# Re-layout reads in 8 transfers per chunk in place of 12, and one transposing transfer per block in place of two

## The chip, the cores and the metric

The kernel runs on 1 core of one Trainium2 chip. The metric is the device time of that core in microseconds (us). The kernel before took 1019.06 us, the median of three runs (1019.06, 1015.35, 1019.22).

## The reference

One transformer block on 2048 tokens of width 640, in float32: a pre-norm attention with 32 heads of 20 over a sliding window of 256 tokens, then a pre-norm GEGLU feed-forward layer of width 1536.

```python
def _A_ref(x, wqkv, wo):
    B, S, D = x.shape
    H = 32; Dh = D // H; W = 256
    qkv = (x @ wqkv).reshape(B, S, 3, H, Dh).transpose(2, 0, 3, 1, 4)
    q, k, v = qkv[0], qkv[1], qkv[2]
    scores = einsum("bhqd,bhkd->bhqk", q, k) * (Dh ** -0.5)
    mask = (idx[:, None] - idx[None, :] >= 0) & (idx[:, None] - idx[None, :] < W)
    p = softmax(where(mask, scores, -1e9))
    o = einsum("bhqk,bhkd->bhqd", p, v)
    return o.transpose(0, 2, 1, 3).reshape(B, S, D) @ wo
...
h = x + _A_ref(layernorm(x), wqkv, wo)
h2 = h + (gelu(layernorm(h) @ w_gate) * (layernorm(h) @ w_up)) @ w_down
```

## The kernel before

**Tiles and parts.** The 2048 tokens are 16 blocks of 128, taken two at a time as 8 chunks of 256 tokens in the attention, and four at a time as 4 chunks in the feed-forward layer. Most products are made from float16 pairs: a value is split into a high part and a low part (what the high part misses), and a product is three matmuls (high by high, high by low, low by high).

**The path of one attention chunk.** `x_lane` normalises a block of x (`layernorm`), and for blocks 4 to 15 `turned` writes its high part (ScalarE) and its low part (VectorE) into one buffer `xp` and turns each with a transposing transfer into `xh` and `xl` (features on partitions). `qk` multiplies with the weights of q or k; `qk_out` splits the result into high and low and ScalarE writes it to a DRAM tile `qk` of [640 features, 2 parts, 256 tokens]. `stack` then reads this tile back in another layout: for each half of the heads (`par`, partitions 0 and 64) it puts three groups of 20 rows below one another, high, high, low for q (`qT`) and high, low, high for k (`kT`), so that one matmul over 60 rows gives all three products. That is 6 transfers of 20 rows x 16 heads x 256 tokens for q and 6 for k, 12 a chunk. Every transfer covers all 16 pairs of heads and both blocks.

**What uses it.** `maxima` multiplies qT with kT to get each row's maximum (VectorE reduces it), the negated maxima go through `max_transpose` as `mT` into rows 60 and 61 of each half of qT (two transfers of 2 rows from ScalarE's queue), `scores` then multiplies over 62 rows, ScalarE takes the exponential, GpSimd masks, and `value_lane` multiplies with v. `wo_block` applies the output weights, adds x, and writes h to DRAM.

**The feed-forward layer.** `norm_lane` reads h back, normalises it, and turns the high and low parts of a block with `turned` into two tiles, `h0h`/`h0l` or `h1h`/`h1l`, for chunks 1 to 3 (chunk 0 is turned on TensorE).

**What sets the order.** All engines' instructions are put in order when the program is built: a list scheduler (`Lane`, the loop at L1632) runs a model of the engines (`Clock`), in which a transfer costs by its bytes, and issues what that model holds ready. On the chip each engine executes its list in order and waits at semaphores. `stack` for chunk c may start once block 2c - 3 is scored (L772), since it overwrites the tiles which that block read, and in the model it keeps its transfers at most `PACE` apart from the line's end. All of its reads, the loads, the transposing transfers and the stores of h are issued by SP, on one queue; ScalarE issues the writes of `qk` and `mT` on another. Eight semaphores go round over the transfers of both queues, so a transfer waits until the one that last had its semaphore has landed.

Of the kernel before, what the change touches and what calls it, by code (L numbers as in the profile page):

```python
# [11 lines left out]
F32 = mybir.dt.float32  # L12
F16 = mybir.dt.float16
# [8 lines left out]
S, D, H, DH, F = 2048, 640, 32, 20, 1536  # L22
P = 128
NB = S // P
KC = D // P
G = 4
HG = H // G
CW = 2 * P
# [3 lines left out]
CB = 4  # L32
# [17 lines left out]
def _pow2(e):  # L50
    return float(2.0 ** e)
# [202 lines left out]
def block_kernel(ctx: ExitStack, tc: tile.TileContext, x, wqkv, wo, wg, wu, wd, out):  # L254
    nc = Clock(tc.nc)
# [3 lines left out]
    ffw = ctx.enter_context(tc.tile_pool(name="ffw", bufs=1))  # L259
# [50 lines left out]
    def need(*reads, slots=(), when=None, eng="tensor"):  # L310

        def f():
            if when and not when() or any(opened[n] >= banks[n] for n in slots):
                return INF
            return max([nc.ready(reads, eng)]
                       + [nc.slot(psums[n], n, banks[n]) for n in slots])
        return f
# [4 lines left out]
    def on(eng, *reads, when=None, after=None):  # L322
        f = need(*reads, when=when, eng=eng)
        if after is not None:
            return (eng,), lambda: max(f(), nc.others(after, eng))
        return (eng,), f
# [142 lines left out]
    def layernorm(xt, lane, hi, lo, dst=None, when=None, xn=None, e=XE, tp="tp",  # L469
                  dma=False):  # L470

        T = lambda n, *shape: nc.tile(lnp, [P] + list(shape), F32, n + lane)
        st = T("lst", 2, 6)
        for i in range(2):
            yield on("vector", xt)
            nc.vector.bn_stats(st[:, i, :], xt[:, i * 320:(i + 1) * 320])
        yield on("vector", st)
        mv = T("lmv", 2)
        nc.vector.bn_aggr(mv, st)
        yield on("vector", mv)  # L480
        ve = T("lve", 1)
        nc.vector.tensor_scalar(ve, mv[:, 1:2], EPS, None, op0=ALU.add)
        yield on("gpsimd", ve)

        y = T("ly", 1)
        a = T("lya", 1)
        nc.gpsimd.tensor_tensor(y, ve, mhalf, op=ALU.pow)
        yield on("vector", y)
        nc.vector.scalar_tensor_tensor(a, y, ve, y, op0=ALU.mult, op1=ALU.mult)
        yield on("vector", a)  # L490
        nc.vector.tensor_scalar(a, a, -0.5 * _pow2(e), 1.5 * _pow2(e), op0=ALU.mult, op1=ALU.add)
        yield on("vector", a)
        nc.vector.tensor_tensor(y, y, a, op=ALU.mult)
        yield on("vector", y)
        xn = xn()
        nc.vector.tensor_scalar(xn, xt, mv[:, 0:1], y, op0=ALU.subtract, op1=ALU.mult)
        if dma is not False:
            yield from turned(xn, lane, (hi, lo), dst, when, dma)
            return
        yield pe(xn, slots=[tp], when=when)  # L500
        if dst:
            hi, lo = dst()
        yield from transpose_part(xn, hi, lo, 0, 4, tp)
        yield pe(xn, slots=[tp])
        yield from transpose_part(xn, hi, lo, 4, 5, tp)

    def turned(src, lane, to, dst=None, when=None, two=None):

        key = "xparts" if dst else "parts"
        yield on("scalar", src, when=lambda: not opened[key] and (not when or when()))  # L510
        opened[key] += 1
        two = (two if dst else lnbuf[2]).bitcast(F16)
        hi, lo = two[:, :D], two[:, D:]
        nc.scalar.copy(hi, src)
        yield on("vector", hi)
        nc.vector.tensor_tensor(lo, src, hi, op=ALU.subtract)
        if dst:
            to = dst()
        for o, i in zip(to, (hi, lo)):
            yield ("sync",), need(i, eng="sync")  # L520
            nc.sync.dma_start_transpose(o, i)
        opened[key] -= 1

    def transpose_part(src, hi, lo, c0, c1, tp="tp"):
# [60 lines left out]
    wq = wqp.enter_context(tc.tile_pool(name="wq", bufs=1, side="right"))  # L585
# [5 lines left out]
    rooms = {"k": gu.bitcast(F32)[:, :KC * D].rearrange("p (c f) -> p c f", f=D)}  # L591
    rooms["k"] = [rooms["k"][:, i] for i in range(KC)]
    x32 = gu.bitcast(F32)[:, KC * D:KC * (D + CW)].rearrange("p (c n) -> p c n", n=CW)
    rooms["v"] = [gu.bitcast(F32)[:, KC * (D + CW):KC * (D + CW) + D]]
    hT = {0: tuple(ffw.tile([P, KC * CB * P], F16, name=n) for n in ("h0h", "h0l"))}
    rooms["v"] += [t.bitcast(F32)[:, i * D:i * D + D] for t in hT[0] for i in range(2)]
    hT[0] = tuple(t.rearrange("p (c n) -> p c n", c=KC) for t in hT[0])
    gu = gu.rearrange("p (a c f) -> p a c f", c=KC, f=512)

    HB = P // 2  # L600
# [55 lines left out]
    def hpart(c, b):  # L656
        return tuple(t[:, :, b * P:(b + 1) * P] for t in hT[c])

    class Block:
        ready = False  # L660
        maxima = halves = v = 0
        h, turned, normed, full = None, False, False, False
# [7 lines left out]
    B = [Block() for _ in range(NB)]  # L670
# [6 lines left out]
    def x_lane(blocks, lane):  # L677

        for j in blocks:
            c = C[j // 2]  # L680
            if j > 1:
                yield on("vector", when=lambda: W["k" if j < NR else "v"].scaled)
            if j >= NR and j + 1 < NB:
                yield ("sync",), lambda: max(0.0, nc.slot(att, "xt", 2))
                load_x(j + 1)

            def dst():
                if j < 2:
                    return x32[:, :, B[j].cols], None
                return xparts(j)  # L690

            yield from layernorm(B[j].x, lane, None, None, dst,
                                 lambda: j < 6 or c.x or C[j // 2 - 3].used == 4,
                                 lambda: B[j].x, tp="rb" if j in (1, 3) else "tp",
                                 dma=j >= NR and at("xp", [P, D], F32, 1))
            if j < 2:
                B[j].full = True
                tasks.append(x_cast(j))
            else:
                B[j].ready = True  # L700

    def xparts(j):
        c = C[j // 2]
        if c.x is None:
            c.x = tuple(nc.tile(wq, [P, KC, CW], F16, n, 3) for n in ("xh", "xl"))
        return tuple(t[:, :, B[j].cols] for t in c.x)

    def x_cast(j):
# [62 lines left out]
    def stack(c, which, d):  # L771
        yield ("sync",), need(d, when=lambda: pos["big"] == 2 and (W["q"].ready if c < 2 else  # L772
                                                                B[2 * c - 3].scored), eng="sync")
        if which == 0:
            C[c].qT = at("qT", [P, H // 2, CW], F16)
            for b in (2 * c, 2 * c + 1):
                B[b].mx = at("mxs", [P, H], F32, 4)
            to = C[c].qT
        else:
            s = 2 * c % RK  # L780
            to = kT[:, :, s:s + 2, :].rearrange("p i r n -> p i (r n)")
        for par in range(2):
            for m, i in enumerate(((0, 0, 1), (0, 1, 0))[which]):
                rows = slice(64 * par + DH * m, 64 * par + DH * m + DH)
                if c > 1:
                    yield ("sync",), lambda: nc.moved["sync"] - PACE
                nc.sync.dma_start(to[rows], d.rearrange("(a d i) m n -> a m d i n", a=2,
                                                        d=DH)[par, i])
        C[c].stacked += 1
        if C[c].stacked == 2:  # L790
            for b in (2 * c, 2 * c + 1):
                for pr in range(0, H // 2, pairs(b)):
                    heapq.heappush(maxq, (b, pr))
# [326 lines left out]
    ffpools = [None, None]  # L1120
# [200 lines left out]
    def norm_start(c):  # L1321
        yield ("sync",), need(when=lambda: pos["gu", c - 2] == FG - 1 if c > 1 else (
            ffpools[0] and W["d", 0].ready and all(b.wrote for b in B[CB:2 * CB])), eng="sync")
        if c == 1:
            hT[1] = tuple(nc.tile(ffpools[0], [P, KC, CB * P], F16, n) for n in ("h1h", "h1l"))
            lnbuf.extend(nc.tile(stage, [P, D], F32, "wsl", SLICES) for _ in range(3))
        else:
            hT[c] = hT[c - 2]
        for i, n in enumerate("hi"):
            side.append((LATE, norm_lane(c, (i, i + 2), n, lnbuf[i])))  # L1330

    def norm_lane(c, bs, lane, t):
        for b in bs:
            j = c * CB + b
            yield ("sync",), lambda: nc.others(t, "sync")
            nc.sync.dma_start(t, h_dram[j * P:(j + 1) * P, :])
            yield from layernorm(t, lane, *hpart(c, b), xn=lambda: t, dma=True,
                                 when=lambda: c < 2 or pos["gu", c - 2] == FG)
            chunk[c] += 1
        if chunk[c] == CB:  # L1340
            side.append((LATE, token_sums(c)))
# [285 lines left out]
    rows = Lane(row_lane())  # L1627
# [89 lines left out]
```

## Time and profile before

| | |
|---|---|
| median of three runs | 1019.06 us |
| the profiled execution, by its own time | 1015.33 us |
| its span, first to last instruction | 1013.6 us |
| mean granted TensorE clock | 0.997 |
| DMA packets; bytes | 105834; 112.67 MB |
| span in which attention runs, read from the first and last uses of kT | 51.8 to 566.3 us |
| transfers qT<-qk and kT<-qk | 48 and 48, 160.0 KB each |
| transposing transfers (x; h) | 24; 24 |

PE is TensorE, PEld its weight loads, DVE VectorE, ACT ScalarE, POOL GpSimd, SP SyncE; a q behind a name (SPq, ACTq) is that engine's instruction queue, here where it issues transfers. Nearly all instructions are recorded by one helper, so all have line L199: groups are told apart by their tiles, written out<-in. A row of the timeline has the start, the time taken, the engine and the instruction, with xN for N merged ones, and in brackets the idle time before it and what ended it. A row of the waits has the total, the count and the longest, in us. A row of the windows has the stretch, its length, the busy time and count of PE, PEld, DVE, ACT and POOL, the granted clock, the mean busy share of the 16 DMA engines, and GB/s.

### The profile page before, as it was taken

How to read it: one execution, taken by the hardware profiler on the slowest of the kernel's cores; microseconds unless marked ns; L12 is line 12 of the kernel's file. 1: busy time of each engine (PE TensorE's matmuls, PEld its weight loads, DVE VectorE, ACT ScalarE, POOL GpSimd, SP SyncE). 2: the span in 40 equal slices, each digit the busy share in tenths (PEclk: the TensorE clock that was granted, in tenths of full speed). 3: DMA queues.
4: the chain of work that ended last, by engine and by line, in shares of the span. 5: the costliest groups of instructions: out<-in, count | busy, mean ns of one | idle time of the engine just before them, and what ended most of it. 6: DMA issues, size and time to landing. Idle time of an engine off the chain costs nothing.

```text
span 1013.6 us, 30516 instructions
## 1 busy us (share of the span) xinstructions
PE 996.3 (98%) x12798; PEld 696.4 (69%) x12798; DVE 754.7 (74%) x2212; ACT 442.5 (44%) x711; POOL 315.0 (31%) x504
## 2 busy tenths in 40 slices
PE   8999999999999999999999999999999999999998
PEld 7876777666666776776655654577777777777776
DVE  7888999786667877676688687798888875544553
ACT  5516666654555555554567634432222212221220
POOL 7004344643344333332345311254313300000000
PEclk9999999999999999999999999999999999999999
DMA  8658775291271714236004342323453542222211
GB/s 308 148 127 177 185 163 167 67 166 41 71 133 39 143 55 88 64 79 188 18 29 133 68 130 92 98 107 116 144 187 102 148 142 78 79 103 80 78 53 52
DMA packets 105834, 112.67 MB, mean 111 GB/s; under 512 B 38368, under 2 KB 79584, under 8 KB 105696
## 3 DMA queue, kind: packets, MB, share of 16 engines
q1 hardware_dynamic: 93600, 99.97, 36.7%
q10 hardware_dynamic: 12096, 10.75, 3.5%
q8 instruction: 100, 1.64, 0.7%
q14 instruction: 38, 0.31, 0.1%
HBM read 73.73 MB, written 28.84 MB: 101 GB/s over the span
## 4 chain that ended last, share of the span: by engine, by line
PE 86%; DVE 7%; DMA 3%; ACT 2%; issue 1%; SPq 1%; POOL 0%; ACTq 0%; DVEq 0%
PE mm L199 44%; PE pv L199 12%; PE ra L199 12%; PE rb L199 10%; PE tp L199 7%; DVE junk L199 1%; DMA kT<-qk 1%; SPq L199 1%; DVE am L199 1%; DMA wst<-in_wu_dram 1%; DMA qT<-in_wqkv_dram 1%; DMA wst<-in_wg_dram 1%; ACT pt L199 1%; DVE ht L199 0%; DVE w1l L199 0%
## 5 line engine op out<-in xcount | busy, mean ns | idle before, releaser
L199 POOL TENSOR_SCALAR_AFFINE_SELECT pt<-pt 128x512 f32<-128x512 f32 x352 | 174.8, 512 | 297.0 <-ACT pt L199 281.3
L199 DVE CUSTOM_DVE_ANT_0 junk<-rb,band 128x320 bf16<-128x320 f32 x228 | 111.5, 489 | 53.4 <-PE rb L199 48.8
L199 ACT ACTIVATE pt<-ra,esc 128x640 f32<-128x640 f32 (+2 forms) x132 | 100.6, 770 | 74.3 <-PE ra L199 69.3
L199 DVE CUSTOM_DVE_ANT_0 junk<-ra,band 128x320 bf16<-128x320 f32 x220 | 107.7, 489 | 33.2 <-PE ra L199 26.8
L199 ACT ACTIVATE pt<-rb,esc 128x640 f32<-128x640 f32 (+2 forms) x124 | 94.1, 764 | 82.4 <-PE rb L199 73.2
L199 PE MATMUL pv<-pt,v 128*21 128x128 f32 x2880 | 104.7, 279 | 0.0
L199 PEld LDWEIGHTS <-ah 128*128 128x128 f16 x768 | 75.1, 98 | 29.2 <-issue 1.9
L199 ACT ACTIVATE gel<-gel,ffk 128x512 f32<-128x512 f32 x36 | 26.0, 722 | 134.3 <-DVE gel L199 134.3
L199 PEld LDWEIGHTS pv<-pt,v 128*21 128x21 f32 x2880 | 70.0, 101 | 9.9 <-issue 1.0
L199 PEld LDWEIGHTS <-ws 128*128 128x128 f16 x720 | 70.5, 98 | 8.1
L199 PEld LDWEIGHTS <-qT 60*64 60x64 f16 x1280 | 29.8, 104 | 61.0 <-issue 51.9
L199 PEld LDWEIGHTS <-kT 62*64 62x64 f16 x2880 | 63.4, 107 | 11.2 <-issue 7.5
L199 PEld LDWEIGHTS <-gu 128*128 128x128 f16 x440 | 41.9, 98 | 36.1 <-issue 2.5
L199 DVE SCALAR_TENSOR_TENSOR ht<-mm,ffk,ht 128x320 f32<-128x320 f32 x96 | 52.1, 545 | 13.7 <-PE mm L199 11.8
L199 ACT CAST ah<-gel 128x512 f16<-128x512 f32 x48 | 29.6, 617 | 68.7 <-DVE gel L199 68.6
L199 PE MATMUL mm<-xh,w1h 128*128 128x256 f16 x200 | 54.6, 273 | 0.8 <-DVE qks L199 0.8
L199 PE MATMUL mm<-xl,w1h 128*128 128x256 f16 x200 | 54.7, 274 | 0.0
L199 PE MATMUL mm<-xh,w1l 128*128 128x256 f16 x200 | 54.6, 273 | 0.0
L199 POOL TENSOR_TENSOR gelt<-gelt 128x256 f32<-128x256 f32 x18 | 15.3, 852 | 112.0 <-ACT gelt L199 111.9
L199 PE MATMUL mm<-w3h,oh 128*128 128x320 f16 x160 | 48.3, 302 | 1.4 <-DVE qks L199 1.4
L199 PE MATMUL mm<-w3l,oh 128*128 128x320 f16 x160 | 48.2, 301 | 0.0
L199 PE MATMUL mm<-w3h,ol 128*128 128x320 f16 x160 | 48.1, 300 | 0.0
(313 smaller groups left out, 2562.6 us busy)
## 6 DMA issues: line engine op xcount, KB each, us to landing
ws<-wsums SPq DMA_DIRECT2D x24, 640.0 KB
qk<-qks ACTq DMA_DIRECT2D x32, 256.0 KB
qT<-qk SPq DMA_DIRECT2D x48, 160.0 KB
kT<-qk SPq DMA_DIRECT2D x48, 160.0 KB
wsums<-ws SPq DMA_DIRECT2D x12, 640.0 KB
ht<-in_x_dram SPq DMA_DIRECT2D x16, 320.0 KB
h_dram<-ht SPq DMA_DIRECT2D x16, 320.0 KB
ht<-h_dram SPq DMA_DIRECT2D x16, 320.0 KB
```

The lines of the kernel that those rows point to most:

```text
L199: r = real(*args, **kw)
```

## The change

`stack` makes 4 transfers in place of 6: of the three groups of 20 rows, two neighbours go as one transfer of 40 rows, the third alone. For q the first two groups are the same source rows (high, high), so the source is read with a leading axis of 2 and step 0; for k they are high and low, so the source is read with the part axis first. The high and low parts of x share one tile `xhl` of 10 slices (the five of `xh`, then the five of `xl`), and those of h one tile `h0` or `h1`, so `turned` issues one transposing transfer of 10 slices after both parts are written, in place of one of 5 slices after each.

```diff
-            yield from turned(xn, lane, (hi, lo), dst, when, dma)
+            yield from turned(xn, lane, hi, dst, when, dma)
...
         if dst:
-            to = dst()
-        for o, i in zip(to, (hi, lo)):
-            yield ("sync",), need(i, eng="sync")
-            nc.sync.dma_start_transpose(o, i)
+            dst()
+            to = dst.all()
+        yield ("sync",), need(two, eng="sync")
+        nc.sync.dma_start_transpose(to, two)
...
+            dst.all = lambda: c.both[:, :, B[j].cols]
...
-            c.x = tuple(nc.tile(wq, [P, KC, CW], F16, n, 3) for n in ("xh", "xl"))
+            c.both = nc.tile(wq, [P, 2 * KC, CW], F16, "xhl", 3)
+            c.x = c.both[:, :KC], c.both[:, KC:]
...
+        parts_ = d.rearrange("(a d i) m n -> a m d i n", a=2, d=DH)
         for par in range(2):
-            for m, i in enumerate(((0, 0, 1), (0, 1, 0))[which]):
-                rows = slice(64 * par + DH * m, 64 * par + DH * m + DH)
+            for m, n in ((0, 2), (2, 1)):
+                rows = slice(64 * par + DH * m, 64 * par + DH * (m + n))
+                if n == 2:
+                    src = parts_[par] if which else parts_[par, 0].unsqueeze(0).to_broadcast(
+                        [2, DH, H // 2, CW])
+                else:
+                    src = parts_[par, 1 - which]
                 if c > 1:
                     yield ("sync",), lambda: nc.moved["sync"] - PACE
-                nc.sync.dma_start(to[rows], d.rearrange("(a d i) m n -> a m d i n", a=2,
-                                                        d=DH)[par, i])
+                nc.sync.dma_start(to[rows], src)
...
-            hT[1] = tuple(nc.tile(ffpools[0], [P, KC, CB * P], F16, n) for n in ("h1h", "h1l"))
+            hB[1] = nc.tile(ffpools[0], [P, 2 * KC, CB * P], F16, "h1")
+            hT[1] = hB[1][:, :KC], hB[1][:, KC:]
...
-            yield from layernorm(t, lane, *hpart(c, b), xn=lambda: t, dma=True,
+            yield from layernorm(t, lane, hB[c % 2][:, :, b * P:(b + 1) * P], None,
+                                 xn=lambda: t, dma=True,
```

SP's rows for chunk 4, in the kernel before; qk_3249 and qk_4034 are the DRAM copies of its q and k, xh and xl the turned x of a later chunk:

```order
L199 DMA qT<-qk_3249 20x16x256 x6
L199 DMA kT<-qk_4034 20x16x256
L199 DMA_TRANSPOSE xh<-xp 128x5x128
L199 DMA_TRANSPOSE xl<-xp 128x5x128
L199 DMA xt<-in_x_dram 128x640
L199 DMA kT<-qk_4034 20x16x256 x5
```

The same place after the change, from the transposing transfer ahead of it; qk_3253 and qk_4019 are now the copies of q and k:

```order
L199 DMA_TRANSPOSE xhl<-xp 128x10x128
L199 DMA ht<-in_x_dram 128x640
L199 DMA xt<-in_x_dram 128x640
L199 DMA qT<-qk_3253 40x16x256
L199 DMA qT<-qk_3253 20x16x256
L199 DMA qT<-qk_3253 40x16x256
L199 DMA qT<-qk_3253 20x16x256
L199 DMA kT<-qk_4019 40x16x256
L199 DMA kT<-qk_4019 20x16x256
L199 DMA kT<-qk_4019 40x16x256
L199 DMA kT<-qk_4019 20x16x256
```

Twelve reads have become eight that alternate between 40 and 20 rows, and the transposing transfers that stood among the reads of k now stand ahead of the whole stack.

ScalarE's rows, with their waits, while chunk 3's stack is in flight after the change: it writes the copy of chunk 4's k (qk_4019) and takes the exponentials (pt) of the blocks in work. DMAHW names the semaphores that go round over all transfers:

```order
L199 DMA qk_4019<-qks 128x2x512 [waits DMAHW2_49,DVE_49]
L199 ACTIVATE pt<-rb,esc 128x2x320 [waits PE_49,Pool_49]
L199 CAST h_100<-tp 128x128 [waits PE_49]
L199 ACTIVATE qks<-mm 128x2x256 [waits DMAHW7_49,PE_49]
L199 ACTIVATE pt<-ra,esc 128x2x320 [waits PE_49]
L199 DMA qk_4019<-qks 128x2x512 [waits DMAHW4_49,DVE_49]
L199 ACTIVATE pt<-rb,esc 128x2x320 [waits PE_49,Pool_49]
L199 ACTIVATE qks<-mm 128x256 [waits DMAHW2_49,PE_49]
L199 ACTIVATE pt<-rb,esc 128x2x320 [waits PE_49]
L199 DMA qk_4019<-qks 128x512 [waits DMAHW7_49,DVE_49]
```

The same rows in the kernel before, from its first write of that copy (qk_4034):

```order
L199 DMA qk_4034<-qks 128x2x512 [waits DMAHW6_49,DVE_49]
L199 ACTIVATE pt<-rb,esc 128x2x320 [waits PE_49,Pool_49]
L199 CAST h0h<-tp 128x128 [waits PE_49]
L199 ACTIVATE pt<-rb,esc 128x2x320 [waits PE_49]
L199 ACTIVATE qks<-mm 128x2x256 [waits PE_49]
L199 ACTIVATE pt<-ra,esc 128x2x320 [waits PE_49,Pool_49]
L199 DMA qk_4034<-qks 128x2x512 [waits DMAHW0_49,DVE_49]
L199 ACTIVATE qks<-mm 128x256 [waits DMAHW6_49,PE_49]
L199 ACTIVATE pt<-rb,esc 128x2x320 [waits PE_49]
L199 DMA qk_4034<-qks 128x512 [waits DVE_49]
```

In both, the writes wait for a transfer that was issued up to eight earlier, and the exponentials behind them stand in the same queue; all three writes have such a wait after the change, two of the three had one in the kernel before.

More of the change, by code (lines that the diff above doesn't have):

```diff
@@ L594, in block_kernel @@
     rooms["v"] = [gu.bitcast(F32)[:, KC * (D + CW):KC * (D + CW) + D]]
-    hT = {0: tuple(ffw.tile([P, KC * CB * P], F16, name=n) for n in ("h0h", "h0l"))}
-    rooms["v"] += [t.bitcast(F32)[:, i * D:i * D + D] for t in hT[0] for i in range(2)]
-    hT[0] = tuple(t.rearrange("p (c n) -> p c n", c=KC) for t in hT[0])
+    h0 = ffw.tile([P, 2 * KC * CB * P], F16, name="h0")
+    rooms["v"] += [h0.bitcast(F32)[:, i * D:i * D + D] for i in range(4)]
+    hB = {0: h0.rearrange("p (c n) -> p c n", c=2 * KC)}
+    hT = {0: (hB[0][:, :KC], hB[0][:, KC:])}
     gu = gu.rearrange("p (a c f) -> p a c f", c=KC, f=512)
```

## The prediction

> **What bounds the kernel now.** First the page: engine shares and the chain that ended last.
>
> ```profile
> span 1013.6 us, 30516 instructions
> PE 996.3 (98%) x12798; PEld 696.4 (69%) x12798; DVE 754.7 (74%) x2212; ACT 442.5 (44%) x711; POOL 315.0 (31%) x504
> PE 86%; DVE 7%; DMA 3%; ACT 2%; issue 1%; SPq 1%; POOL 0%; ACTq 0%; DVEq 0%
> ```
>
> TensorE is busy for 996.3 of 1013.6 us and carries 86% of the chain. It executes its rows in order and the change leaves its matmuls as they are, so the time can fall only by what PE waits, 17.3 us of idle time at most, but it can rise by any wait that is put in. So next the list of PE's own waits, for those that end with a transfer.
>
> ```profile
> PE rb L199 <- DMA kT<-qk: 2.1, 1, 2.1
> PE ra L199 <- DMA kT<-qk: 1.4, 1, 1.4
> ```
>
> Both are the re-layout reads (a stack: qT and kT from their DRAM copy) that the change regroups; no row there names a transposed tile. The timelines show one of them, of chunk 4 (SP's queue, then PE).
>
> ```profile
> 272.21 4.72 SPq L199 DMA_DIRECT2D qT<-qk  x6
> 276.98 0.74 SPq L199 DMA_DIRECT2D kT<-qk  x1
> 279.12 1.24 SPq L199 DMA_TRANSPOSE xh<-xp  x1
> 280.99 1.64 SPq L199 DMA_TRANSPOSE xl<-xp  x1
> 283.31 9.72 SPq L199 DMA_DIRECT2D kT<-qk  x5
> ```
>
> ```profile
> 295.62 0.32 PE L199 MATMUL ra<-kT,qT 60*64 60x320 f16 x1
> 297.31 0.33 PE L199 MATMUL ra<-kT,qT 60*64 60x320 f16 x3 [1.37 <-DMA kT<-qk]
> ```
>
> SP starts reading chunk 4 at 272.21. PE's first maxima matmul of it stands 23.4 us later and still waits 1.37 us. So this stage has cover: PE work between the start of the stack and its first use. Every transfer covers all 16 head pairs, so the first maxima need all of them. The same distance for the first and last of the six chunks 2 to 7, and for chunk 0:
>
> ```profile
> 29.43 5.47 SPq L199 DMA_DIRECT2D qT<-qk  x6
> 51.81 0.31 PE L199 MATMUL ra<-kT,qT 60*64 60x128 f16 x8
> 119.78 3.16 SPq L199 DMA_DIRECT2D qT<-qk  x4
> 159.46 0.38 PE L199 MATMUL ra<-kT,qT 60*64 60x320 f16 x4
> 449.08 4.71 SPq L199 DMA_DIRECT2D qT<-qk  x6
> 476.56 0.33 PE L199 MATMUL rb<-kT,qT 60*64 60x320 f16 x4
> ```
>
> Chunk 2 has 39.7 us and chunk 7 27.5; read the same way, chunks 3 to 6 have 26.6, 23.4, 27.5 and 20.0. Together 164.7, less the waits in chunk 4: 162. In the changed order chunk 2 loses a few us of it, so I take 160.
>
> **The new transfers: how many DMA engines?** A transfer's speed hangs on how many of the 16 DMA engines it uses. Windows (last columns: granted clock, DMA share, GB/s) in which one kind moves nearly alone, and the issues behind the second and third:
>
> ```profile
> 6.00:8.00 2.00, 2.00 (x26) 2.00 (x25) 1.32 (x6) 0.48 (x1) 1.87 (x3) 1.00 1.01 358
> 42.00:43.00 1.00, 1.00 (x6) 0.71 (x5) 0.53 (x2) 0.48 (x2) 0.00 (x0) 1.00 0.60 170
> 160.90:161.80 0.90, 0.90 (x11) 0.81 (x9) 0.87 (x4) 0.79 (x2) 0.00 (x0) 1.00 0.08 18
> 397.00:403.00 6.00, 6.00 (x131) 4.10 (x131) 4.36 (x15) 3.47 (x6) 2.01 (x5) 1.00 0.78 124
> 40.14 4.83 SPq L199 DMA_DIRECT2D kT<-qk  x6
> 159.64 1.28 ACTq L199 DMA_DIRECT2D qT<-mT  x2
> ```
>
> At 6 us the first loads, of 128 rows, fill all engines (1.01, 358 GB/s). At 42 stack reads of 20 destination rows from 320 source rows hold 0.60, just under 10/16. At 160.9 the two mT writes, 32 source rows to 2 destination rows, hold 0.08, under 2/16. So a transfer is cut into equal shares along its outermost rows, and the side with the fewer rows decides: 128 gives 16, 20 and 320 give 10, 2 and 32 give 2. The diff builds the 40-row transfers with 40 destination rows but a source whose outermost count is 2 (a broadcast of two copies, or the m axis put first). By that reading they run on **two engines**. If destination rows alone decided, 40 would give 10 as before; the trace has no source smaller than its destination to settle it. I take two, as the small side decided in the mT row.
>
> The Trainium skill (DMA: Bandwidth & Descriptors, section "Why a DMA increments its semaphore by 16 and not by 1") says that the largest number up to 16 is taken that divides the slowest dimension of both sides; the 10 and the 2 above agree, and by it the new transfers have two engines.
>
> **The sum.** One pass of q or k now is 40, 20, 40, 20 rows with 16 runs of 512 B each. The two engines get 320 + 32 + 320 + 32 = 704 runs each; before, an engine got 6 x 32 = 192. The price of a run: 170 GB/s over 10 engines is 17 GB/s each, 512 B in 30 ns (42 us); 124 GB/s gives 41 ns when several transfers press (397 us); the mT pair, 16 KB in 0.9 us over two engines, gives 28 ns for 256 B. I take 30, nearest to two engines that write different rows; 28 and 41 are the bounds. So q and k need 2 x 704 x 30 ns = 42 us. With 2 us from issue to the first bytes and landing (mT: issued at 159.64, moving at 160.9) and an estimated 4 us of other traffic on the same two engines (0 to 6), a stack takes 48 us.
>
> - Chunks 2 to 7: the stack may start only when the block that last read its buffers is scored, a fixed place in PE's order, so a stall of one chunk doesn't widen the next one's cover. 6 x 48 - 160 = **128 us**.
> - Chunk 0: 29.43 + 48 = 77.4 against a first use at 51.81: **26 us**.
> - Chunk 1: its transfers queue behind chunk 0's on the two engines till about 76, then take 42 + 2: 120. Its first use (88.8 before, 37.0 after chunk 0's) would come at 114: **6 us**.
> - Clock: after chunk 4's wait PE ran a stretch at half clock:
>
> ```profile
> 297.60:301.00 3.40, 3.40 (x78) 2.42 (x67) 1.00 (x4) 0.79 (x1) 1.42 (x3) 0.50 0.74 199
> ```
>
> 3.4 us at 0.50 lose 1.7. Eight long stalls at about 2 us each: **16 us** (0 to 27).
> - Given back: the old kT waits, 2.1 + 1.4, and their 1.7: **-5 us**.
>
> Sum +171. The profiled execution took 1015.33 us, 1.7 beyond its span: 1186. The median of the runs shown, 1019.06, stands 0.4% above that execution; I forecast by the latter.
>
> With 28 ns, no other traffic and no clock loss: a stack 41.4, so 6 x 41.4 - 162 + 19 - 5 = +100. With 41 ns: a stack 66, so 396 - 160 + 44 + 20 + 27 - 5 = +322. These are the bounds, 1115 and 1337.
>
> **The parts costed at nothing.** SP's issues:
>
> ```profile
> L199 SPq DMA_DIRECT2D kT<-qk x48: 742/742/1563, 40.1 to 468.5; - x48
> L199 SPq DMA_TRANSPOSE xh<-xp x12: 1214/1388/2211, 46.0 to 349.5; - x12
> ```
>
> 32 fewer reads at 0.74 us and 24 fewer transposes at 1.4 save SP up to 57 us, less what the larger ones cost more (nothing to double). PE gets none of it: SP's issues run ahead of the bytes. A joined transpose moves the same bytes; its high part now waits for VectorE's low part, and the two issues were 1.9 us apart (279.12, 280.99), so one turning shifts by at most 1.9 us either way. PE never waited for a turned tile; without that cover 24 x 1.9 = 45 us. What queues behind the slow reads on SP (xt, ht, weights) is needed a block or more later. ScalarE's writes of the next qk also wait for landings in the same window of eight semaphores, and its exponentials stand behind them: rival B.
>
> **Rivals.**
> A. *Ten engines* (0.13), the other side: the new reads keep 10 engines because destination rows decide. Then the stack lands no later, chunk 4's wait and half clock go, and 1015.3 - 5.2 gives 1010 (1006 to 1019). For it: the 20-row row fits this reading too. Against it: the mT row, unless only destinations count. It decides at eight engines: with n of them a stack takes 77/n + 10 us (2560 runs shared by n, 128 as before, at 30 ns, and the 6 us above), 48 at two and 20, the smallest cover, at eight. The Trainium skill (same page, "Rules for kernel authors") advises joining many small transfers into one large one; by that alone this would be the outcome.
> B. *Two engines, and ScalarE held as well* (0.11): its qk writes wait for the 20-row reads that queue behind the 40-row ones, so about half of the cover runs after the landing instead of beside it: 1186 + 80 = 1266. For it: the waits in the order rows. Against: most of these writes stand late in the cover.
> C. *Mostly hidden* (0.04): two engines, but far more cover than counted, 1015 to 1085. The distances above speak against it.
>
> **How the numbers follow.** Forecast 0.72 at 1186, its own range 1115 to 1337; B lies within, A and C outside. The range 1095 to 1335 holds a little over 8 in 10. A measurement tells about 0.5% (5 us) from no change. A is split about evenly at that line: faster 0.06, same 0.08 (with a little of C), slower 0.86.
>
> **What would show it.** Right: in the windows right after a stack's issue a DMA share near 0.12 and some 35 GB/s for tens of us; PE's waits named kT<-qk or qT<-qk, eight of 6 to 30 us, each followed by a stretch at clock 0.5; the feed-forward stage after the last chunk as long as before. Wrong: a share near 0.6 during the stack, PE waits as before, and a span within 10 us. If PE waits for exponentials or qk tiles instead, rival B is at work.

## The result, and the profile after

The changed kernel takes **1190.71 us** (median of 6 runs, 1189.80 to 1193.33) against 1015.38 us for the kernel before in the same session (median of 6 runs). The ratio is 1.1718 with a 95% interval of 1.1692 to 1.1745: 17% slower. The prediction was 1186. Two single executions, one of 3413.85 us in experiment 8 and one of 1309.3 us of the kernel before measured beside it, lay far from all others of their kernels, and the ratios leave them out.

First the page of the changed kernel, the same lines as of the kernel before: span, busy time of the engines, the chain that ended last by engine.

```profile
span 1188.0 us, 30424 instructions
PE 1018.7 (86%) x12798; PEld 706.9 (60%) x12798; DVE 750.4 (63%) x2212; ACT 444.0 (37%) x711; POOL 312.8 (26%) x504
PE 63%; SPq 15%; DMA 12%; DVE 6%; ACT 2%; issue 1%; POOL 0%; ACTq 0%; DVEq 0%; POOLq 0%
```

The span grew by 1188.0 - 1013.6 = 174.4 us. PE executes the same 12798 matmuls. Its idle time is now 1188.0 - 1018.7 = 169.3 us where it was 17.3, so 152.0 us of the growth are waits; the other 22.4 us are busy time (1018.7 - 996.3), matmuls that ran slower. Of the chain, 27% now lie on SP's queue and the transfers (4% before), and PE's part fell from 86% to 63%. The list of PE's waits names what ended them (total, count, longest).

```profile
PE rb L199 <- DMA kT<-qk: 47.0, 6, 10.0
PE ra L199 <- DMA kT<-qk: 45.1, 5, 13.2
PE rb L199 <- ACT pt L199: 24.9, 4, 9.3
PE tp L199 <- ACT oT L199: 16.4, 1, 16.4
PE rb L199 <- DVE mxs L199: 9.3, 1, 9.3
PE ra L199 <- ACT pt L199: 7.0, 3, 6.4
```

The two kT waits, 3.5 us before, are 92.1 us now. Beside them stand waits for ScalarE and VectorE that hardly existed before. Windows tell how fast the transfers run: three stretches in which hardly anything but chunk 0's stack moves, then the feed-forward stage after the attention. The last three columns are granted clock, DMA share and GB/s.

```profile
43.00:45.00 2.00, 2.00 (x9) 1.43 (x8) 1.68 (x2) 2.00 (x5) 0.00 (x0) 1.00 0.14 39
45.00:47.00 2.00, 2.00 (x9) 1.42 (x8) 1.62 (x2) 1.14 (x3) 0.00 (x0) 1.00 0.14 43
53.00:55.00 2.00, 0.00 (x0) 0.00 (x0) 0.25 (x1) 0.00 (x0) 0.00 (x0) 1.00 0.14 44
740.00:1188.00 448.00, 442.63 (x3295) 307.16 (x3293) 315.67 (x657) 123.07 (x190) 92.36 (x94) 1.00 0.32 105
```

A share of 0.14 is 2.2 of 16 engines, at 17 to 20 GB/s each. Before, reads of this tile held 0.60 and 170 GB/s. In the feed-forward stage PE is idle for 448.00 - 442.63 = 5.4 us, as little as at the end of the kernel before, by its window:

```profile
575.00:1013.60 438.60, 433.20 (x3068) 300.14 (x3066) 307.33 (x631) 113.82 (x176) 87.21 (x80) 1.00 0.32 104
```

So the loss lies in the attention.

How one chunk shows it: SP's queue around chunk 4's stack (start, time taken), then PE's two waits in it, then a window behind the second.

```profile
360.74 18.49 SPq L199 DMA_DIRECT2D qT<-qk  x4
379.27 20.11 SPq L199 DMA_DIRECT2D kT<-qk  x4
```

```profile
384.71 0.48 PE L199 MATMUL ra<-qT,kT 62*64 62x128 f16 x12 [6.42 <-ACT pt L199]
394.98 0.44 PE L199 MATMUL rb<-kT,qT 60*64 60x320 f16 x1 [5.52 <-DMA kT<-qk]
```

```profile
394.60:401.40 6.80, 0.44 (x1) 0.12 (x1) 0.00 (x0) 0.00 (x0) 0.00 (x0) 0.50 0.22 58
```

The stack is issued at 360.74 and its first maxima start at 394.98; PE waits 6.42 us for an exponential and 5.52 for kT, then waits again, at a granted clock of 0.50. Six issues of q took SP 4.72 us before; four now take 18.49. Put together for all chunks, the windows from each stack's first issue to 20 us after its first maxima, of which the first two, the last, and the sum of the eight:

```profile
29.10:84.70 55.60, 33.05 (x276) 25.12 (x274) 24.18 (x89) 14.20 (x30) 1.65 (x3) 0.79 0.33 72
87.20:145.40 58.20, 38.78 (x439) 24.78 (x437) 27.98 (x120) 16.58 (x35) 8.94 (x12) 0.79 0.48 111
...
606.30:660.40 54.10, 37.82 (x613) 25.50 (x611) 20.54 (x78) 15.82 (x27) 9.77 (x21) 0.84 0.38 116
sum 453.60, PE 296.78 PEld 207.04 DVE 216.40 ACT 151.62 POOL 95.66; mean PE 37.10 PEld 25.88 DVE 27.05 ACT 18.95 POOL 11.96
```

Length less PE's busy time is its idle time: 22.6 us for chunk 0, 19.4 for chunk 1, 16.3 for chunk 7, and 453.60 - 296.78 = 156.8 for all eight, nearly all of the 169.3.

### The profile page after: what moved, and what is told of

Read it like the earlier page. It is cut to its first block, busy times and chain, and to the rows that moved or that the text cites. A ratio compares the mean times of both kernels' runs of the same rounds, so it can differ in the third digit from the quotient of the medians.

```text
span 1188.0 us, 30424 instructions
## 1 busy us (share of the span) xinstructions
PE 1018.7 (86%) x12798; PEld 706.9 (60%) x12798; DVE 750.4 (63%) x2212; ACT 444.0 (37%) x711; POOL 312.8 (26%) x504
## 4 chain that ended last, share of the span: by engine, by line
PE 63%; SPq 15%; DMA 12%; DVE 6%; ACT 2%; issue 1%; POOL 0%; ACTq 0%; DVEq 0%; POOLq 0%
PE mm L199 31%; SPq L199 15%; PE ra L199 9%; PE pv L199 9%; DMA kT<-qk 8%; PE rb L199 8%; PE tp L199 6%; DMA qT<-qk 2%; DMA xhl<-xp 1%; DVE junk L199 1%; DMA wsl<-in_wg_dram 1%; DVE ts L199 1%; DVE am L199 1%; ACT pt L199 1%; DVE w1l L199 0%
## 5 line engine op out<-in xcount | busy, mean ns | idle before, releaser
L199 DVE CUSTOM_DVE_ANT_0 junk<-rb,band 128x320 bf16<-128x320 f32 x214 | 104.7, 489 | 98.3 <-PE rb L199 93.0
L199 DVE CUSTOM_DVE_ANT_0 junk<-ra,band 128x320 bf16<-128x320 f32 x234 | 114.5, 489 | 82.3 <-PE ra L199 76.7
L199 PE MATMUL rb<-kT,qT 60*64 60x320 f16 (+4 forms) x616 | 40.8, 286 | 49.6 <-DMA kT<-qk 47.0
L199 PE MATMUL ra<-kT,qT 60*64 60x320 f16 (+4 forms) x664 | 44.1, 291 | 45.1 <-DMA kT<-qk 45.1
L199 PE MATMUL mm<-xhl,w1h 128*128 128x256 f16 x400 | 75.4, 282 | 1.2 <-DVE qks L199 1.2
L199 PE MATMUL rb<-qT,kT 62*64 62x128 f16 x1488 | 41.7, 214 | 34.2 <-ACT pt L199 24.9
L199 PE MATMUL mm<-xhl,w0h 128*128 128x256 f16 x350 | 66.8, 282 | 0.0
L199 PE MATMUL mm<-w2h,xhl 128*128 128x320 f16 x280 | 66.3, 316 | 0.0
L199 PE MATMUL mm<-h,gu 128*128 128x512 f16 (+1 forms) x272 | 65.8, 386 | 0.0
L199 PE MATMUL mm<-xhl,w1l 128*128 128x256 f16 x200 | 56.3, 282 | 0.0
```

Source lines behind the costliest of these rows:

```text
L199: r = real(*args, **kw)
```

## The experiments

The theory from the start: a 40-row read of the stack whose source has outermost count 2 runs on two DMA engines, and PE waits for the stack. Its main rivals: the joined reads are slow for another reason (their size, the order on SP's queue, the step-0 axis of q alone); the joined transposing transfers have a part; ScalarE, held by its writes, adds its own time. Ratios are to the kernel before, measured on the same chip in the same session.

**1. The joined reads alone.** `turned` and the tiles are those of the kernel before, `stack` is that of the change:

```diff
-        yield ("sync",), need(two, eng="sync")
-        nc.sync.dma_start_transpose(to, two)
+        for o, i in zip(to, (hi, lo)):
+            yield ("sync",), need(i, eng="sync")
+            nc.sync.dma_start_transpose(o, i)
...
```

> Only the joined re-layout reads, the turning transfers as before. Theory (a read whose source has an outermost count of 2 runs on two DMA engines, so a stack takes about 48 us): 1175 to 1205 us, and PE waits of about 20 us in each of the eight chunks. Rival (the joined transposing transfers are part of the loss): under 1170 us.

Measured: 1188.97 us (2 runs), ratio 1.1699 (1.1663 to 1.1736). The reads alone make the whole loss.

**2. The joined transposing transfers alone.** `stack` is that of the kernel before, with 12 reads:

```diff
-            for m, n in ((0, 2), (2, 1)):
+            for m, i in enumerate(((0, 0, 1), (0, 1, 0))[which]):
...
```

> Only the joined transposing transfers, the reads in 12 transfers of 20 rows as before. Theory: 1008 to 1020 us, the same as before within 0.5%. Rival (the joined turning delays x or h): over 1025 us.

Measured: 1010.66 us (6 runs), ratio 0.9944 (0.9924 to 0.9963), 0.6% below the kernel before: little, but the interval leaves out 1. The page of this kernel, and its waits for kT:

```profile
PE 992.2 (98%) x12798; PEld 694.6 (69%) x12798; DVE 750.8 (74%) x2212; ACT 444.5 (44%) x711; POOL 313.5 (31%) x504
```

```profile
PE rb L199 <- DMA kT<-qk: 1.7, 2, 1.2
PE ra L199 <- DMA kT<-qk: 0.3, 1, 0.3
```

Of the 4.7 us that the span lost (1013.6 to 1008.9), 4.1 are busy time of PE (996.3 to 992.2). The kernel before ran two stretches of 3.4 us at half clock, one after each kT wait of over a microsecond; the first of them:

```profile
229.55 0.32 PE L199 MATMUL rb<-kT,qT 60*64 60x64 f16 x3 [2.14 <-DMA kT<-qk]
```

```profile
229.30:232.70 3.40, 3.15 (x50) 1.77 (x50) 1.00 (x4) 0.79 (x1) 0.00 (x0) 0.50 0.03 7
```

The kernel with joined turning alone is at clock 1.00 from start to end. In it the six reads of chunk 4's k are issued one behind the other, where in the kernel before two transposing transfers and a load stood between the first and the rest. That the gain comes from this is read from the queue and not tested by itself.

**3. Only k's reads joined** (k in 4 transfers, q in 6; turning joined as in the change):

```diff
-            for m, n in ((0, 2), (2, 1)):
+            for m, n in (((0, 2), (2, 1)) if which != 0 else ((0, 1), (1, 1), (2, 1))):
...
```

> The changed kernel with the reads of k joined (source with the part axis first, no step of 0) and those of q in 6 transfers again. Theory: the two engines get 704 runs of k and 192 of q a chunk, 21 + 8 us, with 2 us of start and 4 of other traffic 35 us; six chunks 6 x 35 - 160 = 50, chunk 0 13, clock 8 to 16, less 5: 1075 to 1105 us. Rival (the source read twice with step 0 is what is slow, so only q's reads): 1010 to 1025 us.

Measured: 1104.71 us (2 runs), ratio 1.0870 (1.0836 to 1.0904). k's source has no step-0 axis (its part axis is real), so the loss does not need the broadcast.

**4. A layout in which a 40-row read has 40 rows outermost.** The DRAM copy becomes [half of the heads, part, 320 features, 256]; the three groups are put in the order high, low, high for q and low, high, high for k, so that a read takes two parts that lie behind one another. A copy is then written in 6 pieces in place of 3.

```diff
-        d = dram.tile([D, 2, CW], F16, name=f"qk{c}{which}")
+        d = dram.tile([2, 2, D // 2, CW], F16, name=f"qk{c}{which}")
...
-                nc.sync.dma_start(to[rows], src)
+                nc.sync.dma_start(to[rows], src.rearrange("m (d i) n -> (m d) i n", d=DH))
```

> The changed kernel with the DRAM copy laid out as [half, part, 320 features, 256 tokens] and k's parts stored low first, so that each 40-row read has one source of 640 (k) or 40 (q) outermost rows; the groups of q become high, low, high and those of k low, high, high. Still 8 transfers a chunk, 4 of 40 rows. ScalarE writes the copy in 6 transfers in place of 3. Theory (the outermost count of 2 is the cause): ten engines again, no stall of 20 us, 1005 to 1020 us. Rival (a 40-row transfer, or fewer and larger transfers, is slow in itself): 1150 us or more.

Measured: 1072.44 us (6 runs), ratio 1.0559 (1.0531 to 1.0587): neither of the two. The long kT waits were gone, but the page shows another program:

```profile
PE 1030.2 (97%) x13318; PEld 728.8 (68%) x13318; DVE 751.7 (70%) x2212; ACT 442.3 (41%) x711; POOL 315.0 (30%) x504
```

520 matmuls more, and PE busy for 97% of the span. They multiply by the identity into `pv`: the scheduler fills idle time of its model with them, and three further writes in the model had made it plan such time at the start. The run could not be read as a test of the reads.

**5. The same layout with the changed kernel's order.** The transfers are issued past the scheduler's model, and the model is told of the old ones, so that PE, VectorE and SP execute their instructions in the changed kernel's order:

```diff
+        put = nc.scalar.real.dma_start
+        if ts[0] == 0:
+            for t in range(2):
+                put(d[0, :, t * P:t * P + P].rearrange("m p n -> p m n"), st[:, t])
...
+        nc.issue("scalar", nc.scalar.cost("dma_start", old, [both]), [both], [old], 0.4)
```

> The changed kernel with one thing undone: the DRAM copy is laid out as [half of the heads, part, 320 features, 256], so that a 40-row read has 40 rows outermost on both sides (ten engines by theory); the copy is written in 6 pieces per q or k in place of 3, and the order of all other instructions is that of the changed kernel exactly (TensorE executes 12798 matmuls again, not 13318 as in the first version of this layout). Theory (the outermost count of 2 is the loss): the stalls after each stack go, the clock is back near 1.0, 1005 to 1025, within 1% of the kernel with the joined transposing transfers alone (1010.7). Rival (joined reads are slow for another reason: their size, 8 transfers in place of 12, the order of SP's queue with the turning ahead of the stack): 1150 or more. Second rival (the loss of the first version, 1072, came from the six writes themselves and not from the order that the scheduler made of them): 1060 to 1080 again.

Measured: 1020.37 us (12 runs), ratio 1.0046 (1.0026 to 1.0066). The page, the first of PE's waits, and SP's issues of chunk 4 (L803 is the read in this kernel's own file):

```profile
PE 993.7 (98%) x12798; PEld 695.4 (68%) x12798; DVE 752.3 (74%) x2212; ACT 442.8 (43%) x711; POOL 314.1 (31%) x504
```

```profile
PE rb L199 <- ACT pt L199: 5.5, 7, 1.3
PE ra L199 <- ACT pt L199: 2.9, 5, 1.1
```

```profile
273.28 1.52 SPq L803 DMA_DIRECT2D qT<-qk  x4
277.10 7.35 SPq L803 DMA_DIRECT2D kT<-qk  x4
```

Eight reads, half of them of 40 rows, in the same order, and 170 us of the 1190.7 are gone: kT is no longer among these waits, and SP is free again after 1.52 and 7.35 us. The rest of 10 us against experiment 2 is 1.5 us of busy time and 8.3 us of idle time, and PE's waits for exponentials are 8.2 us longer. ScalarE, which issues twice as many writes of the copy, is held behind them in the row below; that the six writes cause the rest is read from this and not tested by itself:

```profile
302.11 0.60 ACTq L775 DMA_DIRECT2D qk<-qks  x1
302.81 1.06 ACTq L777 DMA_DIRECT2D qk<-qks  x1
303.97 0.79 ACT L199 ACTIVATE pt<-rb,esc 128x640 f32<-128x640 f32 x1 [2.59 <-DMA qk<-qks]
```

**6. Only q's reads joined** (experiment 3 the other way round; like it, with the joined turning, which the expectation leaves out):

```diff
-            for m, n in ((0, 2), (2, 1)):
+            for m, n in (((0, 2), (2, 1)) if which == 0 else ((0, 1), (1, 1), (2, 1))):
...
```

> The kernel before, with q's reads joined (source read with a leading axis of step 0) and k's left in 6. Theory (704 runs of 512 B per engine for q alone, 21 us and 6 more, plus k's 12 us, in place of 48): a stack of some 35 to 40 us, 1075 to 1110, as with k alone joined (1104.7). Rival (the step-0 axis costs nothing extra, k's part axis alone is slow): 1015. Rival (the step-0 axis is the slow one): 1150 or more.

Measured: 1102.52 us (4 runs), ratio 1.0863 (1.0820 to 1.0905). From experiment 2's 1010.7, q alone adds 91.8, k alone 94.0, both 180.0 (the changed kernel): the two nearly add up (185.8), and neither the step-0 axis nor the part axis is special.

**7. The copy's writes from GpSimd**, so that no exponential stands behind them:

```diff
-        nc.scalar.dma_start(d[ts[0] * P:(ts[-1] + 1) * P].rearrange("(t p) m n -> p t (m n)", p=P),
-                            both)
+        to = d[ts[0] * P:(ts[-1] + 1) * P].rearrange("(t p) m n -> p t (m n)", p=P)
+        nc.gpsimd.real.dma_start(to, both)
+        nc.issue("scalar", nc.scalar.cost("dma_start", to, [both]), [both], [to], 0.4)
```

> The changed kernel, with the three writes of each DRAM copy issued by GpSimd in place of ScalarE, so that no exponential stands behind a write that waits for the landing of a slow read; the order of TensorE, VectorE and SP is unchanged. Theory (the stack itself, 48 us against a cover of 20 to 40, sets the loss; ScalarE's waits lie inside it): the waits named pt and mxs turn into waits named kT, the total stays, 1165 to 1205. Rival B of the prediction (ScalarE's held queue adds its own time): half of the stall goes, 1090 to 1140. GpSimd's masks stand behind the writes instead; if they are held the same way the total stays too, and the waits would be named pt.

Measured: 1190.80 us (4 runs), ratio 1.1731 (1.1694 to 1.1769), the same as the changed kernel. Chunk 4 goes as expected. First ScalarE in the changed kernel, held by the write of the copy, then PE in this one:

```profile
383.40 0.37 ACTq L199 DMA_DIRECT2D qk<-qks  x1
383.87 0.79 ACT L199 ACTIVATE pt<-ra,esc 128x640 f32<-128x640 f32 x1 [7.56 <-DMA qT<-qk]
```

```profile
395.25 0.44 PE L199 MATMUL rb<-kT,qT 60*64 60x320 f16 x1 [13.50 <-DMA kT<-qk]
```

PE's 6.42 us for the exponential are gone there, it does that work earlier, and then waits 13.50 us for kT in place of 5.52. The maxima start at 395.25 in place of 394.98, so in this chunk ScalarE's wait lay inside the stack's time and added nothing. The expectation that the waits for pt and mxs would all turn into waits for kT did not come true. The rows for the whole kernel, the last of them ScalarE's own:

```profile
PE rb L199 <- DMA kT<-qk: 57.6, 6, 13.5
PE ra L199 <- DMA kT<-qk: 42.5, 5, 13.0
PE rb L199 <- ACT pt L199: 30.7, 4, 12.3
ACT xp L199 <- DMA xhl<-xp: 66.5, 4, 25.3
```

PE still waits 30.9 us for exponentials, where it was 31.9. ScalarE, free of the writes, is now held before it fills xp, by transposing transfers that stand behind the reads on SP's queue (27.6 us of such waits in the changed kernel, 66.5 here). The experiment clears the writes; it does not take ScalarE out of the chain.

**8. and 9. Layout, length of the runs, and outermost count taken apart.** The layout of experiment 5 changed two things more: q's reads became runs of 8 KB (k's stay at 512 B, since kT is not contiguous) and the writes became six. Experiment 8 keeps all of that and puts 16 unused rows behind each part, so that the source of a 40-row read is [2, 20, 4096] for q and [2, 320, 256] for k, and no longer [40, 4096] and [640, 256]. Experiment 9 puts 256 unused elements behind each feature row, so that all runs are 512 B again, while the rows of the two parts still follow at one step ([640, 256] for both). The first lines of the two edits against experiment 5, 8 first (the slices that follow from them are not shown):

```diff
-        d = dram.tile([2, 2, D // 2, CW], F16, name=f"qk{c}{which}")
+        d = dram.tile([2, 2, D // 2 + 16, CW], F16, name=f"qk{c}{which}")
...
```

```diff
-        d = dram.tile([2, 2, D // 2, CW], F16, name=f"qk{c}{which}")
+        dd = dram.tile([2, 2, D // 2, 2 * CW], F16, name=f"qk{c}{which}")
+        d = dd[:, :, :, :CW]
...
```

> The kernel of e5_wide8_same_order with 16 unused feature rows behind each part of the DRAM copy, so that the two parts of a 40-row read no longer follow one another without a gap and its source has outermost count 2 again; writes, order and sizes of the runs are those of e5 (q's reads in runs of 8 KB, k's in runs of 512 B). Theory (outermost count 2 puts the read on two engines): the loss comes back. k alone gave 87 us, and q's 8 KB runs may cost less per byte than 16 runs of 512 B: 1100 to 1200, DMA share near 0.12 in the stacks. Rival (e5 was fast because of its larger runs or its layout): 1010 to 1030.

> The kernel of e5_wide8_same_order with 256 unused elements behind each feature row of the DRAM copy, so that every run of every read is 512 B again as in the changed kernel, while a 40-row read keeps 40 rows outermost on both sides. Theory (the number of engines): the stalls stay away, 1005 to 1035. Rival (e5 was fast because q's runs were 8 KB): q's share of the loss comes back, 1090 to 1120.

Measured: 1171.90 us (4 runs), ratio 1.1510 (1.1454 to 1.1566), and 1020.52 us (10 runs), ratio 1.0054 (1.0026 to 1.0081). With the changed kernel, which alone of the four writes the copy in three pieces, and experiment 5 this makes a square:

| source's outermost count of a 40-row read | all runs 512 B | q's runs 8 KB |
|---|---|---|
| 2 | 1190.7 (the change) | 1171.9 (8) |
| 40 or 640 | 1020.5 (9) | 1020.4 (5) |

The rows of the table are 150 to 170 us apart, its columns at most 19. An unused gap between two parts costs 150 us. A window in chunk 0's stack of experiment 9, then the same of the changed kernel, in both with other traffic beside the reads:

```profile
35.00:37.00 2.00, 2.00 (x13) 1.63 (x12) 1.93 (x9) 0.20 (x1) 0.00 (x0) 1.00 0.85 221
35.00:37.00 2.00, 2.00 (x12) 1.51 (x11) 1.90 (x9) 0.00 (x0) 0.00 (x0) 1.00 0.42 139
```

The packet records of the traces set the stack apart, since its runs alone have 512 B on SP's queue. From its first run to its last a stack takes 14.7 to 23.9 us in experiment 9 and 38.4 to 46.6 in the changed kernel.

## Why the prediction was right, step by step

- **PE is the bound, with little to win.** Right. The best kernel of the study wins 5.7 us, and the change lost through PE's waits (152.0 us) and the slower clock behind them (22.4).
- **Two engines.** Right, and the step that decides: share 0.14 where 0.12 was said, 39 to 44 GB/s where some 35 were said, and the square above. The Trainium skill (DMA: Bandwidth & Descriptors, section "Rules for kernel authors") says that a leading broadcast axis of c copies confines a transfer to at most c engines. These windows agree for c = 2; experiment 3 shows the same loss for a part axis of count 2 with a real step.
- **Price and length of a stack: 30 ns a run, 48 us.** About right. In the packet records of the trace a 512 B run takes 27 ns in the median and 31.5 in the mean. From SP's first issue to the end of the last run a stack takes 40.5 to 48.1 us, 44.5 in the mean over eight chunks. The 4 us for other traffic were too many.
- **The cover: 160 us.** Two readings in it are off, by a few us. The first maxima do not need all reads: they use one half of the heads, and the second half is waited for by itself (in chunk 0 of the change 13.23 us and then 9.31). And the waits taken off lie behind the first maxima, where the distances end; the one of 2.14 us is chunk 3's.
- **Chunk 0: 26 us.** 22.6 by the window. **Chunks 2 to 7: 128 us.** 156.8 - 22.6 - 19.4 = 114.8 by the windows. The shorter stack explains the sign: 6 x 3.5 = 21 us less, of which 13 are seen.
- **Chunk 1: 6 us. This step failed**: 19.4. It let chunk 1's transfers start on time and queue behind chunk 0's on the two engines, and let PE come late to them. In fact the copy itself came late. From the timelines, the last two writes of chunk 1's q on ScalarE's queue and its first reads on SP's, of the kernel before and then of the changed one:

```profile
59.59 2.77 ACTq L199 DMA_DIRECT2D qk<-qks  x2
61.82 6.16 SPq L199 DMA_DIRECT2D qT<-qk  x6
```

```profile
84.94 2.01 ACTq L199 DMA_DIRECT2D qk<-qks  x2
87.21 18.53 SPq L199 DMA_DIRECT2D qT<-qk  x4
```

PE stood still at chunk 0's first maxima and then ran at half clock, and the products for chunk 1 come behind these in its order. They came 25 us late, the stack was issued at 87.21 in place of 61.82, and chunk 1 had the same distance to its first use as any other chunk, so it paid like one. A stall does not shorten the next stack's wait if the data of that stack are made by the stalled engine.
- **Clock: 16 us.** 22.4 by PE's busy time, inside the 0 to 27 that were given.
- **Given back: -5 us.** Not visible in the change, where the stacks are slow; the turning alone gives 5.7 (experiment 2).
- **The sum.** 22.6 + 19.4 + 114.8 + 22.4 = 179.2, less 4.8 of idle time elsewhere (17.3 before, 169.3 - 156.8 = 12.5 now), is the 174.4 of the spans. It was 171: chunk 1 and the clock were 20 us too small, and chunks 0 and 2 to 7 were 17 us too large. The closeness owes something to these errors being of opposite signs.
- **Costed at nothing.** The joined turning as such: right for the change (experiment 1 against it, 1189.0 and 1190.7), but not in general, since alone it wins 5.7 us. The issues saved on SP: the instructions were fewer, but SP saved no time, as its queue is held by the slow reads (18.49 and 20.11 us for four); SPq is 15% of the chain now. **A third term, what queues behind the slow reads on SP, was wrong**: it was said to be needed a block or more later. In chunk 2 ScalarE stands 10.41 us for a load of weights, and PE behind it 8.97 us for an exponential:

```profile
ACT gu L199 <- DMA wsl<-in_wg_dram: 10.4, 1, 10.4
```

```profile
226.08 0.48 PE L199 MATMUL rb<-qT,kT 62*64 62x128 f16 x12 [8.97 <-ACT pt L199]
230.37 0.45 PE L199 MATMUL ra<-kT,qT 60*64 60x320 f16 x4
```

The last run of this chunk's stack ended at 224.11, 6.3 us before its first maxima. In the other seven chunks PE's last wait is for kT and ends 0.6 to 1.2 us after the last run. So the holding adds an estimated 5 us, in chunk 2 alone; no run takes it away by itself.
- **Rival A** (ten engines) is out. With joined reads that do run on more engines (5 and 9) the kernel still came out 10 us behind the one with 12 reads (2), and the six writes of the layout that they need are the likely reason. **Rival B** was seen in part and is out as a price of 80 us: ScalarE is held and PE waits 31.9 us for its exponentials, but without the writes in its queue (experiment 7) the time is the same. What holds it then, loads and transposing transfers, is not what the rival named, and in seven of eight chunks PE waits for kT afterwards all the same. **Rival C** is out by the windows of the eight chunks.

## What to carry to other kernels

Before two transfers are joined into a larger one, look at the outermost counts of both sides as they will be written: a join that puts a count of 2 outermost makes one transfer of two, and runs it on two of 16 engines. If a join is wanted, lay the source out so that the rows to be joined follow one another at one step and can be written as one axis, and count what that layout costs where it is written. A new wait inside the time of a transfer that is waited for anyway adds nothing; ask for each wait what the engine would meet next without it.

## What the runs showed that had not been expected

- SP's own queue is held by the confined transfers: eight issues take 38.6 us for chunk 4, against 8.87 when the same rows are read on more engines (experiment 5), and everything behind them on that queue waits. The confinement alone does not do it: in experiment 8 q's reads are confined too, but in 16 times fewer and longer runs, and their four issues are done in 2.98 us where k's, in 512 B runs, take 17.71 (chunk 1).

```profile
83.35 2.98 SPq L803 DMA_DIRECT2D qT<-qk  x4
104.78 17.71 SPq L803 DMA_DIRECT2D kT<-qk  x4
```

- On two engines, 8 KB runs were not much better than 512 B runs: q's reads in 16 times longer runs saved 19 us of the 92 that joining them adds (experiments 8 and 6), with six writes of the copy in place of three beside them.
- Two waits of 1.37 and 2.14 us before were each followed by 3.4 us at a granted clock of 0.50, a loss of 1.7 us each beside the wait itself. The kernel of experiment 2, whose longest wait for kT is 1.2 us, has no such stretch. The length of a wait does not settle it alone: in experiment 2 PE also waits 1.85 us for VectorE, in the feed-forward stage, and the clock stays at 1.00.
